# Moving the first loads of a fused attention and two-layer MoE kernel within the program's order

## The chip, the cores and the metric

The kernel runs on one core of one Trainium2 chip. The metric is the device time of one execution in microseconds (us). The program before took 1236.12 us (median of three runs, 1235.98 to 1238.45).

Engines, as the profile names them: PE is TensorE's matrix multiply and PEld its weight load, DVE is VectorE, ACT is ScalarE, POOL is GpSimd, SP is SyncE, which here issues nearly all DMA transfers.

## The reference, cut

Attention with normalized queries and keys over 4 batches and 12 heads of 448 positions and 64 channels, then two feed-forward layers on the 1792 tokens of 768 channels:

```python
def attention(q, k, v, g_q, g_k):                    # (4, 12, 448, 64)
    q_n, k_n = rmsnorm(q, g_q), rmsnorm(k, g_k)      # x / sqrt(mean(x*x) + 1e-6) * g
    s = q_n @ k_n.T / 8
    p = exp(s - max(s)); p = p / (sum(p) + 1e-9)
    return p @ v
x = tokens(attention(...))                           # (1792, 768)
x = relu(x @ w_in) ** 2 @ w_out                      # 768 -> 2048 -> 768
y = ((x @ w1) * (x @ w2)) @ w3 @ w_out2              # 768 -> 1024 -> 1024 -> 768
```

The feed-forward weights arrive as 64-bit floating-point words. The kernel multiplies w3 and w_out2 first (the product is called w3o) and then uses the product as one matrix.

## The kernel before, in words

**Passes.** The main loop (L676) runs over 48 heads in four passes of 12, one pass for each batch. While a pass computes the attention of its heads, a generator gives out matmuls that fill TensorE between them: in the first pass `gen_w3o` (the product w3o), in the later ones `gen_moe` of the batch before. `fill(n)` takes about n matmuls from the generator; six calls of it stand in each turn of the loop.

**Weight units.** The weights are cut into units of 128 rows and 384 or 512 columns, 384 to 512 KB as 64-bit words. For each unit there is a load (L180, buffer raw64, four of them), `words` (on ACT the exponent part, L194; the low word on POOL, L200, or every third unit in the first pass on ACT, L198), `join` on DVE (L207), `split_hi` on ACT (the fp32r half, L106) and `split_lo` on POOL or, every fifth unit in the first pass, on DVE (the rest, L114). `mm3` (L262 to L264) then makes three matmuls for each weight block and operand: high by high, high by low, low by high. In the first product both operands are such units: unit 0 is from w3, units 1 to 4 are from w_out2 and are kept in tiles x and act, unit 5 is from w3 again. `advance` gives out the steps some units ahead: loads five units ahead, words three, joins two.

**Heads.** Four heads are a group. `load_group` loads natural-order keys kn (two buffers) and queries qn (one buffer) of a group; `group_prep` makes their sums of squares (ACT L450, DVE L452) and reciprocal roots (DVE L428 to L434, tile rr). `load_head` loads one head's transposed queries qt (two buffers), `load_v` its values. `head_prep` makes kx and its halves khl on POOL, qh on ACT and ql on DVE (L496). `stage_k` transposes the keys (L508), `stage_qk` makes scores for half a head and their maxima (L524 to L527, tile nb), `stage_exp` the exps on ACT (L543), `stage_t` and `stage_lo` the transposed probabilities, `stage_v` the product with the values.

**Order.** The text of the program gives each instruction its rank; the framework then plans one queue for each engine from ranks, readiness and free buffers, and each engine works through its queue in order, waiting where it must. So an instruction that is ready early may stand ahead of the program's text, and a load stands in SP's queue behind others that wait.

**The start.** L661 to L675: the gains, group 0 (with the first head's keys and queries and units 0 and 1 in between, L397 to L403), the second head's queries (L663), then `group_prep(0)`, the third head's queries (L671), `head_prep(1)` and the first values (L673). The first turn of the loop issues the fourth head's queries, the second values and group 1 (L678 to L681), and only the `fill` at L683 reaches unit 2.

Of the kernel before, what the change touches and what calls it, by code (L numbers as in the profile page):

```python
# [29 lines left out]
def attention_moe_kernel(  # L30
# [19 lines left out]
    GH = 4  # L50
# [120 lines left out]
    def is64(i):  # L171
        return units[i][0].dtype != F32
# [14 lines left out]
    def load_to(i):  # L187
        while pos["load"] <= min(i, NU - 1) and is64(pos["load"]):
            load_next()
# [200 lines left out]
    def load_group(g):  # L390
        if not (0 <= g < NH // GH):
            return
        b, h0 = divmod(g * GH, H)
        qn = t1.tile([P, GH, C, D], F32, name="qn", tag="qn")
        kn = t2.tile([P, GH, C, D], F32, name="kn", tag="kn")
        if g == 0:
            nc.sync.dma_start(out=kn[:, 0:1], in_=k_nat[0, :, 0:1])  # L397
            load_head(0)
            nc.sync.dma_start(out=qn[:, 0:1], in_=q_nat[0, :, 0:1])
            load_to(0)  # L400
            nc.sync.dma_start(out=kn[:, 1:], in_=k_nat[0, :, 1:GH])
            nc.sync.dma_start(out=qn[:, 1:], in_=q_nat[0, :, 1:GH])
            load_to(1)  # L403
        else:
            nc.sync.dma_start(out=kn, in_=k_nat[b, :, h0:h0 + GH])
            nc.sync.dma_start(out=qn, in_=q_nat[b, :, h0:h0 + GH])
        grp[g] = [qn, kn, None, None]

    def load_head(h):
        if not (0 <= h < NH):  # L410
            return
        b, hh = divmod(h, H)
        t = t2.tile([128, S], F32, name="qt", tag="qt")
        nc.sync.dma_start(out=t, in_=q_t[b, hh])
        qts[h] = t

    def load_v(h):
        if not (0 <= h < NH):
            return
        b, hh = divmod(h, H)  # L420
        t = t2.tile([128, C, D], F32, name="v", tag="v")
        nc.sync.dma_start(out=t, in_=v_in[b, hh])
        vs[h] = t
# [105 lines left out]
    def stage_exp(h, s):  # L529
        if not (0 <= h < NH):  # L530
            return
        d = heads[h]
        nb, o = d.pop("nb"), d.pop("sc")
        i = h % 2
        if s == 0 and i == 0:
            sums2[h // 2] = small.tile([P, 2, C], F32, name="sm", tag="sm")
        sm = sums2[h // 2]
        c0 = 2 * s
        pp = t3.tile([P, 2, S], F32, name="p", tag="p")
        for j in range(2):  # L540
            c = c0 + j
            p = d["p"][c] = pp[:, j, :]
            nc.scalar.activation(  # L543
                out=p, in_=o[j], func=AF.Exp, scale=d["rq"][:, c:c + 1], bias=nb[:, j:j + 1],
                accum_out=sm[:, i, c:c + 1],
            )
        if h >= H:
            words = t3.tile([P, 2, S], F32R, name="pw", tag="pw")
            nc.sync.dma_start(out=words.bitcast(F32), in_=pp)
            d["p"][c0:c0 + 2] = [words[:, 0, :], words[:, 1, :]]  # L550
        if s == 1 and i == 1:
            nc.vector.tensor_scalar(out=sm, in0=sm, scalar1=1e-9, scalar2=None, op0=ALU.add)
            rs = small.tile([P, 2, C], F32, name="rs", tag="rs")
            nc.vector.reciprocal(out=rs, in_=sm)
            wide = t1.tile([P, C, 2, D], F32, name="rsw", tag="rsw")
            nc.gpsimd.tensor_scalar(
                out=wide, in0=rs.rearrange("p i c -> p c i").unsqueeze(3).to_broadcast([P, C, 2, D]),
                scalar1=1.0, scalar2=1.0, op0=ALU.mult, op1=ALU.mult,
            )
            sums2[h // 2] = wide.rearrange("p c i d -> p c (i d)")  # L560
# [84 lines left out]
    def start_fill(gen, total):  # L645
        state.update(gen=gen, credit=0.0, left=total)
# [14 lines left out]
    nc.sync.dma_start(out=g_sb, in_=g_in)  # L661
    load_group(0)
    load_head(1)  # L663
    make_identity(nc, ident)
    nc.vector.tensor_copy(out=ident_r, in_=ident)
    nc.vector.scalar_tensor_tensor(
# [8 lines left out]
    first.close()  # L675
    for h in range(NH + 1):  # L676
        n = W3O / ((H + 1) * 6) if h <= H else MOE / (H * 6)
        load_head(h + 3)  # L678
        load_v(h + 1)
        if h % GH == 0:  # L680
            load_group(h // GH + 1)  # L681
        stage_qk(h, 0)
        fill(n)  # L683
        stage_exp(h, 0)
        if h % H != 1:
            stage_x(h - 2)
        stage_t(h - 1, 0)
        stage_t(h - 1, 1)
        fill(n)
        stage_lo(h - 1)  # L690
        if h < NH:
            v_prep(h)
        fill(n)
        stage_k(h + 1)
        stage_t(h - 1, 2)
        stage_t(h - 1, 3)
        fill(n)
        stage_lo(h - 1)
        stage_qk(h, 1)
        fill(n)  # L700
        stage_exp(h, 1)
        fill(n)
        stage_v(h - 1)
        if h % GH == 1:
            group_prep(h // GH + 1)
        head_prep(h + 2)
        if h and h % H == 0:
            fill(1e9)
            stage_x(h - 1)
            start_fill(gen_moe(h // H - 1), MOE)  # L710
# [57 lines left out]
```

## Time and profile before

| | us |
|---|---|
| median of three runs | 1236.12 |
| the profiled execution | 1234.55 |
| its span, first to last instruction | 1232.8 |
| PE busy in the span | 1160.9 (94%) |
| ACT busy | 728.5 (59%) |
| DVE busy | 709.7 (58%) |
| POOL busy | 781.3 (63%) |

A share over the whole span says little here: the first 450 us (the start, the first pass and most of the second) and the rest have different limits. A table of stretches shows for each stretch how long each engine was busy, the granted clock of TensorE and how busy the DMA engines were. A table of waits shows for one engine what released it and how long it stood idle for that. A timeline shows single instructions with start, duration, and, in brackets, idle time before them with what ended it.

### The profile page before, as it was taken

The page shows a single profiled execution, that of the slowest core. Times are in us where ns is not written, and L with a number is a line of the kernel's source. Part 1 is how long each engine was busy: PE and PEld are TensorE (multiplying, and loading weights), DVE is VectorE, ACT ScalarE, POOL GpSimd, SP SyncE. Part 2 cuts the span into 40 slices and gives each one's busy share as a digit, 9 for nine tenths or more (in the row PEclk, how much of TensorE's full clock was granted, in tenths as well). Part 3 has the DMA queues.
Part 4 walks back from the last instruction along what each step waited for, and adds up shares of the span by engine and source line. Part 5 has one row for each costly group of instructions (what it writes and reads, how often), then busy time and mean ns, then how long its engine had stood idle before and what let it go on. Part 6 is the DMA issues. An engine that isn't in the chain of part 4 may idle for free.

```text
span 1232.8 us, 18950 instructions
## 1 busy us (share of the span) xinstructions
PE 1160.9 (94%) x6192; PEld 1049.3 (85%) x6192; DVE 709.7 (58%) x1314; ACT 728.5 (59%) x1553; POOL 781.3 (63%) x772
## 2 busy tenths in 40 slices
PE   3789999998989899999999999999999999999998
PEld 2578888886878789998998998999999999999998
DVE  6699879768978774646567555655664421012100
ACT  5889876767657565656645555656545554343342
POOL 5875534655676655766776764856766556678673
PEclk9999999999998999999999999999999999999999
DMA  7774557888888755555535455544544443333342
GB/s 218 244 238 151 165 146 226 276 283 264 251 264 257 234 180 179 146 148 145 151 118 161 139 169 158 143 142 127 154 123 120 138 138 113 107 116 102 104 125 75
DMA packets 111347, 207.63 MB, mean 168 GB/s; under 512 B 12208, under 2 KB 66704, under 8 KB 111248
## 3 DMA queue, kind: packets, MB, share of 16 engines
q1 hardware_dynamic: 107792, 200.92, 54.0%
q10 hardware_dynamic: 3456, 5.51, 1.2%
q8 instruction: 49, 0.80, 0.3%
q14 instruction: 50, 0.41, 0.1%
HBM read 149.95 MB, written 27.53 MB: 144 GB/s over the span
## 4 chain that ended last, share of the span: by engine, by line
PE 60%; DMA 4%; DVE 2%; POOL 2%; ACT 1%; issue 1%; SPq 0%; DVEq 0%; POOLq 0%; ACTq 0%
PE mm L262 17%; PE mm L263 17%; PE mm L264 17%; PE kv L622 3%; PE pt L570 3%; DMA raw<-w 2%; DMA pw<-p 2%; PE sc L525 1%; PE sc L524 1%; POOL hl L114 1%; DVE raw L207 1%; PE kv L508 1%; PE mm L611 0%; ACT p L543 0%; POOL x L114 0%
## 5 line engine op out<-in xcount | busy, mean ns | idle before, releaser
L114 POOL TENSOR_TENSOR hl<-raw,hl 128x384 fp32r<-128x384 f32 (+1 forms) x383 | 446.4, 1169 | 258.5 <-ACT hl L106 253.3
L106 ACT ACTIVATE hl<-raw 128x384 fp32r<-128x384 f32 (+1 forms) x416 | 233.7, 564 | 147.6 <-PE mm L264 85.6
L263 PE MATMUL mm<-x,hl 128*128 128x448 f32 (+1 forms) x832 | 306.2, 368 | 8.6 <-POOL x L114 8.6
L262 PE MATMUL mm<-x,hl 128*128 128x448 f32 (+1 forms) x832 | 310.5, 373 | 3.8 <-ACT x L106 1.8
L264 PE MATMUL mm<-x,hl 128*128 128x448 f32 (+1 forms) x832 | 305.7, 367 | 4.5 <-POOL hl L114 2.6
L263 PE MATMUL mm<-act,hl 128*128 128x448 f32 (+1 forms) x640 | 234.4, 366 | 3.3 <-POOL act L114 3.2
L262 PE MATMUL mm<-act,hl 128*128 128x448 f32 (+1 forms) x640 | 236.9, 370 | 0.0
L264 PE MATMUL mm<-act,hl 128*128 128x448 f32 (+1 forms) x640 | 233.6, 365 | 0.7 <-DVE hl L114 0.7
L543 ACT ACTIVATE p<-sc,nb,rr 112x448 f32<-112x448 f32 x192 | 137.4, 719 | 86.4 <-DVE nb L527 83.0
L263 PEld LDWEIGHTS mm<-x,hl 128*128 128x128 f32 x832 | 158.1, 190 | 22.1 <-POOL x L114 10.2
L264 PEld LDWEIGHTS mm<-x,hl 128*128 128x128 f32 x832 | 158.2, 190 | 19.0 <-POOL hl L114 4.0
L262 PEld LDWEIGHTS mm<-x,hl 128*128 128x128 f32 x832 | 157.9, 190 | 18.5 <-ACT x L106 3.3
L526 DVE TENSOR_REDUCE nb<-sc 112x1 f32<-112x448 f32 x192 | 113.1, 615 | 35.6 <-PE sc L525 34.3
L263 PEld LDWEIGHTS mm<-act,hl 128*128 128x128 f32 x640 | 121.0, 189 | 14.3 <-POOL act L114 4.8
L264 PEld LDWEIGHTS mm<-act,hl 128*128 128x128 f32 x640 | 120.9, 189 | 10.6 <-DVE hl L114 1.1
L262 PEld LDWEIGHTS mm<-act,hl 128*128 128x128 f32 x640 | 121.0, 189 | 9.4
L114 DVE TENSOR_TENSOR ptr<-pt,ptr 128x448 fp32r<-128x448 f32 x144 | 87.1, 619 | 72.0 <-ACT ptr L106 71.4
L200 POOL TENSOR_SCALAR raw<-raw 128x384 uint32<-128x384 uint16 (+1 forms) x110 | 82.1, 747 | 73.0 <-DMA raw<-w_in 18.8
L207 DVE SCALAR_TENSOR_TENSOR raw<-raw 128x384 uint32<-128x384 uint32 (+1 forms) x120 | 84.8, 711 | 39.8 <-POOL hl L114 25.2
L194 ACT ACTIVATE raw<-raw 128x384 f32<-128x384 f32 (+1 forms) x120 | 70.5, 597 | 53.9 <-DMA raw<-w 18.0
L114 POOL TENSOR_TENSOR act<-gf,act 128x448 fp32r<-128x448 f32 x80 | 97.4, 1218 | 7.2 <-DVE gf L334 3.0
L334 DVE TENSOR_TENSOR gf<-mm,r 128x448 f32<-128x448 f32 x64 | 39.8, 621 | 94.4 <-ACT r L330 93.9
(82 smaller groups left out, 1588.7 us busy)
## 6 DMA issues: line engine op xcount, KB each, us to landing
pw<-p SPq DMA_DIRECT2D x72, 392.0 KB, 4.3
raw<-f_in SPq DMA_DIRECT2D x96, 192.0 KB, 2.4
raw<-f_out SPq DMA_DIRECT2D x72, 256.0 KB, 2.7
raw<-f SPq DMA_DIRECT2D x96, 192.0 KB, 2.4
raw<-w_in SPq DMA_DIRECT2D x32, 384.0 KB, 4.5
raw<-w_out SPq DMA_DIRECT2D x24, 512.0 KB, 6.1
raw<-w SPq DMA_DIRECT2D x32, 384.0 KB, 4.9
raw<-w3o SPq DMA_DIRECT2D x48, 256.0 KB, 2.7
```

What stands on the lines that cost most here:

```text
L106: nc.scalar.activation(out=out, in_=in_, func=AF.Copy)
L114: e.tensor_tensor(out=out, in0=in0, in1=in1, op=ALU.subtract)
L194: nc.scalar.activation(out=hi, in_=hi, func=AF.Prelu, scale=2.0**-112, alpha=-(2.0**32))
L200: nc.gpsimd.tensor_scalar(out=t[:, :n, 0], in0=low, scalar1=2.0**-13, scalar2=2.0**-14 - 0.5, op0=ALU.mult, op1=ALU.add)
L207: nc.vector.scalar_tensor_tensor(out=f[:, :n].bitcast(U32), in0=t[:, :n, 1], scalar=3, in1=t[:, :n, 0], op0=ALU.logical_shift_left, op1=AL ...
L262: nc.tensor.matmul(ps, w[:, 0, wk, :], x[0], start=(i == 0), stop=False)
L263: nc.tensor.matmul(ps, w[:, 0, wk, :], x[1], start=False, stop=False)
L264: nc.tensor.matmul(ps, w[:, 1, wk, :], x[0], start=False, stop=(i == last))
L334: nc.vector.tensor_tensor(out=gf, in0=ps, in1=r, op=ALU.mult)
L526: nc.vector.tensor_reduce(out=nb[:, j:j + 1], in_=o[j], axis=AX.X, op=ALU.max, negate=True)
L543: nc.scalar.activation(out=p, in_=o[j], func=AF.Exp, scale=d["rq"][:, c:c + 1], bias=nb[:, j:j + 1], accum_out=sm[:, i, c:c + 1],)
L570: nc.tensor.transpose(to[:kn, c * P:(c + 1) * P], d["p"][c][:, k0:k0 + kn], one)
```

## The change

Four places in the program's text:

- units 2 and 3 are loaded directly behind the second head's queries (`load_to(3)`);
- in the first turn of the loop the second values, group 1 and the fourth head's queries are issued behind `stage_exp(0, 0)` instead of ahead of `stage_qk(0, 0)`;
- groups from group 2 on are loaded in the turns h = 3, 7, 11, ... instead of 4, 8, 12, ...;
- `head_prep(h + 2)` stands ahead of `group_prep`, no longer behind it.

No instruction is added or taken away.

```diff
@@ -661,6 +661,7 @@
     nc.sync.dma_start(out=g_sb, in_=g_in)
     load_group(0)
     load_head(1)
+    load_to(3)
     make_identity(nc, ident)
@@ -675,13 +676,18 @@
     for h in range(NH + 1):
         n = W3O / ((H + 1) * 6) if h <= H else MOE / (H * 6)
-        load_head(h + 3)
-        load_v(h + 1)
-        if h % GH == 0:
-            load_group(h // GH + 1)
+        if h:
+            load_head(h + 3)
+            load_v(h + 1)
+            if h % GH == 3:
+                load_group(h // GH + 2)
         stage_qk(h, 0)
         fill(n)
         stage_exp(h, 0)
+        if h == 0:
+            load_v(1)
+            load_group(1)
+            load_head(3)
         if h % H != 1:
             stage_x(h - 2)
@@ -701,9 +707,9 @@
         stage_v(h - 1)
+        head_prep(h + 2)
         if h % GH == 1:
             group_prep(h // GH + 1)
-        head_prep(h + 2)
         if h and h % H == 0:
             fill(1e9)
```

## Rows read from the trace of the kernel before

**Rows 1.** Stretches: us; each engine's busy time (instructions), clock, DMA share, GB/s.

```profile
10.00:20.00 10.00, 3.81 (x10) 2.06 (x10) 9.61 (x31) 4.14 (x9) 5.04 (x6) 1.00 0.92 276
20.00:30.00 10.00, 4.76 (x18) 3.04 (x18) 5.24 (x9) 6.62 (x14) 9.08 (x13) 1.00 0.49 164
30.00:60.00 30.00, 21.25 (x87) 15.96 (x88) 20.15 (x33) 24.41 (x55) 24.79 (x25) 0.94 0.77 243
60.00:120.00 60.00, 54.18 (x329) 48.20 (x327) 58.67 (x112) 53.39 (x114) 41.13 (x47) 1.00 0.63 197
...
180.00:450.00 270.00, 242.11 (x1265) 214.65 (x1265) 219.09 (x398) 176.97 (x386) 163.35 (x177) 0.97 0.80 250
450.00:1230.00 780.00, 777.40 (x4135) 713.25 (x4133) 343.13 (x612) 411.31 (x869) 508.38 (x463) 1.00 0.46 134
```

**Rows 2.** Waits of PE, 0 to 60 us: total us, times, longest us.

```profile
PE mm L263 <- POOL x L114: 7.3, 4, 2.9
PE sc L524 <- ACT p L543: 3.4, 1, 3.4
PE mm L263 <- POOL act L114: 3.2, 4, 1.7
PE mm L262 <- ACT x L106: 1.8, 1, 1.8
```

**Rows 3.** Timeline of PE: start us, duration us, engine, line, operation, [idle before, releaser].

```profile
29.95 0.69 PE L263 MATMUL mm<-x,hl 128*128 128x384 f32 x1 [2.91 <-POOL x L114]
```

**Rows 4.** Timeline of SP's issues, first 17 us.

```profile
4.47 2.85 SPq L414 DMA_DIRECT2D qt<-q_t  x2
...
8.32 0.44 SPq L405 DMA_DIRECT2D kn<-k_nat  x1
12.24 0.32 SPq L406 DMA_DIRECT2D qn<-q_nat  x1
...
14.96 1.37 SPq L180 DMA_DIRECT2D raw<-wo  x3
```

**Rows 5.** Timeline of ACT, 18 to 64 us.

```profile
18.99 0.72 ACT L543 ACTIVATE p<-sc,nb,rr 112x448 f32<-112x448 f32 x1 [5.68 <-DVE nb L527]
...
23.04 0.54 ACT L194 ACTIVATE raw<-raw 128x384 f32<-128x384 f32 x1
...
25.80 0.51 ACT L106 ACTIVATE x<-raw 128x384 fp32r<-128x384 f32 x1
...
63.43 1.05 ACT L450 ACTIVATE qn<-kn 112x1024 f32<-112x1024 f32 x1
```

**Rows 6.** Timeline of POOL, 10 to 20 us.

```profile
10.66 0.68 POOL L200 TENSOR_SCALAR raw<-raw 128x384 uint32<-128x384 uint16 x1 [1.20 <-DMA raw<-wo]
...
14.01 1.37 POOL L114 TENSOR_TENSOR x<-raw,x 128x384 fp32r<-128x384 f32 x1
17.16 1.58 POOL L114 TENSOR_TENSOR vhl<-v,vhl 128x256 fp32r<-128x256 f32 x2 [1.78 <-DVE nt L432]
19.85 0.61 POOL L480 TENSOR_TENSOR kx<-kn,rr 112x256 f32<-112x256 f32 x1 [1.11 <-issue]
```

**Rows 7.** Timeline of DVE, 6 to 15 us.

```profile
6.29 0.69 DVE L496 SCALAR_TENSOR_TENSOR ql<-qt,gg,qh 128x448 fp32r<-128x448 f32 x1
...
12.20 0.55 DVE L207 SCALAR_TENSOR_TENSOR raw<-raw 128x384 uint32<-128x384 uint32 x1
...
12.83 1.70 DVE L496 SCALAR_TENSOR_TENSOR ql<-qt,gg,qh 128x448 fp32r<-128x448 f32 x1
```

**Rows 8.** Timeline of all engines around a kn load and a group's square.

```profile
85.18 0.63 POOL L480 TENSOR_TENSOR kx<-kn,rr 112x256 f32<-112x256 f32 x1
...
85.84 0.33 SPq L405 DMA_DIRECT2D kn<-k_nat  x1
...
176.22 1.06 ACT L450 ACTIVATE qn<-kn 112x1024 f32<-112x1024 f32 x1 [3.64 <-DMA kn<-k_nat]
...
178.04 0.46 PE L524 MATMUL sc<-kt,qh 128*112 128x448 f32 x1 [1.62 <-ACT p L543]
```

## Prediction

> **What bounds the kernel now.** I read the table of stretches first, then the waits of TensorE (PE) in the stretches where it stands idle, and last the order of each engine's instructions there. The table says where PE idles [rows 1]. From 450 us on it is busy 777.4 of 780 us: no wait of another engine ends last there. From 180 to 450 us it idles 27.9 us, with DMA busy 0.80 of the time. From 60 to 120 us it idles 5.8 us, but VectorE (DVE) is busy 58.67 of 60. From 10 to 60 us it idles 10 − 3.81, 10 − 4.76 and 30 − 21.25, together 20.2 us. The reader should see that in these 50 us no engine is full throughout: DVE is full from 10 to 20 us (9.61 of 10) and about half busy in the next ten, GpSimd (POOL) is half idle from 10 to 20 us (5.04) and full in the next ten (9.08), and ScalarE (ACT) does 4.14 of 10 in the first stretch. Work is short there, then comes all at once.
>
> What is short are weight units. Each unit (64-bit words) is made into an fp32 value and split into two fp32r halves by ACT (exponent, sometimes the low word, high half), POOL (low word, low half) and DVE (join). The waits of PE in the first 60 us that name a unit are 7.3 us for low halves in tile x, 3.2 us for those in tile act and 1.8 us for a high half [rows 2]. The longest, 2.9 us, ends at 29.95 us: it is for unit 2's low half, and the 1.8 us a little earlier for the same unit's high half [rows 2, 3]. Unit 2's load was issued at 14.96 us, behind group 1's two loads at 8.32 and 12.24 us [rows 4]. Its exponent was begun on ACT at 23.04 us, and before that ACT had stood 5.68 us, to 18.99 us, for the first exp's bias [rows 5], and POOL 1.78 and 1.11 us ahead of its work at 17.16 and 19.85 us [rows 6]. Both engines idled with no unit to work on, although two of the four unit buffers had never been used.
>
> **The change, part by part.**
>
> 1. *Units 2 and 3 behind the second head's queries.* Two issues move from 14.96 us to directly behind the first load of the pair at 4.47 us [rows 4]. Queued behind them on SP are now the third head's queries and the first value tile: two issues of about 0.45 us (1.37 us for three [rows 4]), and 768 KB in the data, at the 276 GB/s of the stretch from 10 to 20 us [rows 1] an estimated 2.8 us. Unit 1 lands at 10.66 us, where POOL's wait for it ends [rows 6]; behind it come 224 KB of queries and 384 KB for each unit, so units 2 and 3 land at an estimated 12.9 and 14.3 us, and the third head's queries and the values 1.3 us later, at 15.6 us. The values are read by POOL from 17.16 us on [rows 6]: covered, 0; without that cover up to 2.8 us, on the work on the values alone.
>    What moves into idle time: on ACT two exponents of 0.54 us, one low word, put at the same 0.54, and two high halves of 0.51, together 2.6 us, into the wait of 5.68 us [rows 5]. On POOL one low word of 0.68 and two low halves of 1.37 us, together 3.4 us, against 1.78 + 1.11 = 2.9 us of idle time [rows 6]. On DVE two joins of 0.55 us [rows 7], into a stretch that is already full.
>    POOL is the fullest engine after it (9.08 of 10, then 24.79 of 30 us [rows 1]), so the gain is what POOL does ahead of time: 2.9 us. The bounds: at the top the two waits of PE for unit 2 are all gone, 1.8 + 2.9 = 4.7 us; with units 4 and 5 earlier too (their buffers come free with the joins, the second of which ends at 12.75 us [rows 7], and a group load no longer stands in the queue ahead of them) ACT's whole 5.7 us could be filled. At the bottom, below nothing: the first exp comes later by 3.1 us (rival 2). I take 2.9 us, by the row of the engine that is full next.
>
> 2. *The first pass's loads (values 1, group 1, queries 3) behind its exps.* Their readers don't wait now: group 1's last square lies at 63.43 us with no wait in front [rows 5], 55 us behind the first of the group's loads. SP may have nothing else to issue behind the units, and then part of them goes out where it goes now. Cost 0, covered by those 55 us; uncovered, a group load that lands late holds ACT as it does at 176.22 us, for 3.64 us, and PE 1.62 us at 178.04 us [rows 8]. What it gives, a queue free for units 4 and 5, is already in the bounds of part 1.
>
> 3. *Groups loaded a head ahead, from group 2 on.* A load of kn needs the buffer of the group before last, which the last kx of that group frees: kx at 85.18 us, load at 85.84 us [rows 8], and so for nine of the eleven groups. For these the buffer and not the place in the program sets the time, so 0, and the wait of 3.64 us stays where it is. Only group 2 can go earlier; its squares have no wait in front, so 0.
>
> 4. *head_prep before group_prep.* No instruction more or less; only the rank of some ACT, DVE and POOL work at every fourth head. For this the trace has no row; I take 0, between − 1.6 and + 1.6 us (one wait of PE as at 178.04 us, either way [rows 8]).
>
> Sum: − 2.9 us. From 60 to 120 us DVE is full, so the gain survives only if DVE gets its work earlier too; from 20 to 60 us it is idle 4.8 + 9.9 = 14.6 us [rows 1], so it has the room. After that every stage is the same, begun 2.9 us earlier. Against the profiled execution: 1234.55 − 2.9 = 1231.7 us (its span is 1232.8, with 1.75 us around it). The median of the three runs lies 1.57 us above that execution, so 1236.12 − 2.9 = **1233.2 us**.
>
> **Rivals.**
>
> 1. *The whole head start, faster.* Units 4 and 5 follow at once, ACT's 5.68 us are filled, and POOL is fed without a gap: − 5.7 us, 1230.4. For it: ACT and POOL work on each unit in turn, and ACT has the time. Against it: POOL has only 2.9 us free there.
>
> 2. *The first exp becomes late, slower.* The chain to the first exp ends on DVE, which is full from 10 to 20 us [rows 1]. Two joins put 2 × 0.55 = 1.1 us into it. Besides, DVE slows while POOL works: the operation that makes ql takes 0.69 us at 6.29 us and 1.70 us at 12.83 us [rows 7], where POOL makes low halves (one from 14.01 us [rows 6]). Each of two more low halves ahead of the exp may so cost DVE 1.0 us. The exp would then start at 18.99 + 1.1 + 2.0 = 22.1 us, 3.1 us later. It decides once the waits for the units are gone and the exps of heads 0 and 1 end last before 60 us. Then nothing is won and up to 3.1 us are lost: 1239.2. Against it: of PE's waits up to 60 us only 3.4 us are for an exp [rows 2].
>    The Trainium skill speaks for this rival: SBUF — State Buffer, section "Who interferes with whom", says that a DVE instruction with two SBUF inputs and a GpSimd instruction that reads SBUF exclude each other for the whole instruction. The trace agrees as far as the 1.70 against 0.69 us go. By the rule alone each low half could hold DVE for its whole 1.37 us, which would make the exp an estimated 3.8 us later instead of 3.1.
>
> 3. *Given back.* The units come earlier, but DVE, full from 60 to 120 us, ends its part no earlier: between 0 and − 1 us, 1235.6. For it: 58.67 of 60 [rows 1]. Against it: DVE's 14.6 idle us before.
>
> 4. *A new order later on.* Parts 3 and 4 change the rank of work at every fourth head. Between 180 and 450 us, where PE idles 27.9 us, three more waits as at 178.04 us cost 4.9 us: 1238.1 with the gain of part 1; three fewer would give 1228.3. Nothing in the trace says which.
>
> 5. *It doesn't do what it says.* For the group loads this is the forecast (buffer, not place). For units 2 and 3 it can hardly be, since their buffers are free; it has no chance of its own.
>
> **How the numbers follow.** 0.2% is 2.5 us, about what a measurement of this kernel can tell from no change. Forecast (− 1.5 to − 4.7 us): 0.40, of it 0.29 beyond 2.5 us. Rival 1: 0.13, faster. Rival 2: 0.13, of it 0.10 slower. Rival 3: 0.14, same. Rival 4: 0.20, of it 0.06 faster, 0.02 same, 0.12 slower. Faster 0.29 + 0.13 + 0.06 = 0.48; same 0.11 + 0.03 + 0.14 + 0.02 = 0.30; slower 0.10 + 0.12 = 0.22. The forecast's own range is 1231.4 to 1234.6. The range that holds 8 in 10 goes down past rival 1 towards rival 4's lower end and up past rival 2: 1227 to 1240.
>
> **What would show it.** Right: units 2 and 3 issued near 5 us, their exponents on ACT before 18 us, the low half of unit 2 in use on PE before 25 us instead of at 29.95, POOL busy more than 6.5 of 10 in the stretch from 10 to 20 us, TensorE's idle time from 10 to 60 us down by about 3 us and that of the later stretches as it is. The first exp later than 21 us shows the cost of rival 2. PE idle from 60 to 120 us by more than 7 us, DVE as full as now, shows rival 3. Loads of kn that no longer follow the last kx, or PE idle from 180 to 450 us away from 27.9 us by more than 2 us, show rival 4. The forecast is wrong if PE's idle time from 10 to 60 us does not fall.

## The result: 0.65% slower

The changed kernel takes 1245.56 us (median of 13 runs, 1239.13 to 1248.99) against 1236.18 us for the kernel before (13 runs, 1233.9 to 1243.29): ratio 1.0065, 95% interval 1.005 to 1.0079. The forecast was 1233.2 us with a range of 1227 to 1240; the sign was wrong, and the time lies 5.6 us above the range. The profiled execution of after took 1244.28 us, its span is 1242.4 us.

**The busy times.** Of the 9.6 us between the spans, TensorE's busy time takes 10.6 (1160.9 to 1171.5 us) for the same 6192 matmuls; DVE (709.7), ACT (728.4) and POOL (778.6) are as busy as before or less. The table of stretches of after (columns as in [rows 1]):

```profile
10.00:20.00 10.00, 4.77 (x13) 2.51 (x12) 9.59 (x28) 6.52 (x13) 5.27 (x6) 1.00 0.77 254
20.00:30.00 10.00, 7.14 (x21) 4.87 (x21) 5.71 (x12) 5.98 (x13) 8.99 (x13) 1.00 0.73 242
30.00:60.00 30.00, 18.03 (x65) 12.78 (x65) 17.39 (x29) 20.75 (x46) 19.05 (x20) 0.93 0.57 179
60.00:120.00 60.00, 54.93 (x314) 48.32 (x315) 53.91 (x107) 50.77 (x105) 40.33 (x44) 0.95 0.72 219
120.00:180.00 60.00, 55.23 (x324) 50.03 (x323) 48.58 (x101) 44.63 (x100) 26.97 (x36) 0.94 0.45 130
180.00:450.00 270.00, 244.96 (x1277) 216.45 (x1276) 219.85 (x402) 178.41 (x390) 160.30 (x178) 0.96 0.79 248
450.00:1230.00 780.00, 777.46 (x4142) 713.45 (x4142) 351.05 (x623) 416.33 (x881) 512.95 (x468) 1.00 0.47 137
```

Against [rows 1], TensorE does more up to 30 us (34 matmuls from 10 to 30 us, 28 before), then much less from 30 to 60 us (65, before 87). From 10 to 60 us it idles 5.23 + 2.86 + 11.97 = 20.1 us, before 20.2: the same idle time with 99 instead of 115 matmuls in it. From 120 to 180 us, where the kernel before had

```profile
120.00:180.00 60.00, 56.94 (x355) 51.63 (x354) 49.47 (x108) 47.16 (x106) 26.10 (x35) 1.00 0.53 155
```

after does 31 matmuls less, at a granted clock of 0.94. From 450 us on the rows are alike. (The profile has no record of the clock before its first rise, at 33.8 us in before and 41.9 in after, and the table counts that time as 1.00; the distance of the matmuls shows the lower level there.)

**The start of after.** Issues on SP, work on ACT, POOL, PE and DVE (each with "..." where rows are left out), and one row of SP's waits from 36 to 47 us:

```profile
5.24 1.69 SPq L180 DMA_DIRECT2D raw<-wo  x2
...
36.95 0.33 SPq L180 DMA_DIRECT2D raw<-wo  x1
41.51 0.38 SPq L289 DMA_DIRECT2D w3o<-osb  x1
41.98 0.44 SPq L414 DMA_DIRECT2D qt<-q_t  x1
46.02 2.99 SPq L180 DMA_DIRECT2D raw<-wo  x4
```
```profile
13.70 0.55 ACT L194 ACTIVATE raw<-raw 128x384 f32<-128x384 f32 x1
...
20.16 0.72 ACT L543 ACTIVATE p<-sc,nb,rr 112x448 f32<-112x448 f32 x1 [0.50 <-DVE nb L527]
...
31.61 0.54 ACT L194 ACTIVATE raw<-raw 128x384 f32<-128x384 f32 x1
34.21 0.52 ACT L106 ACTIVATE act<-raw 128x384 fp32r<-128x384 f32 x1 [2.06 <-DVE raw L207]
...
40.99 0.49 ACT L106 ACTIVATE osb<-mm 128x384 f32<-128x384 f32 x1 [2.24 <-PE mm L264]
...
44.16 1.00 ACT L194 ACTIVATE raw<-raw 128x384 f32<-128x384 f32 x2
```
```profile
22.91 0.85 POOL L480 TENSOR_TENSOR kx<-kn,rr 112x256 f32<-112x256 f32 x1 [0.18 <-DVE rr L434]
...
30.21 1.09 POOL L114 TENSOR_TENSOR khl<-kx,khl 112x256 fp32r<-112x256 f32 x1
31.27 1.26 POOL L114 TENSOR_TENSOR hl<-raw,hl 128x512 fp32r<-128x512 f32 x1
32.50 0.99 POOL L114 TENSOR_TENSOR act<-raw,act 128x384 fp32r<-128x384 f32 x1
...
40.19 1.07 POOL L200 TENSOR_SCALAR raw<-raw 128x384 uint32<-128x384 uint16 x1 [0.96 <-DMA raw<-wo]
47.22 2.30 POOL L114 TENSOR_TENSOR act<-raw,act 128x384 fp32r<-128x384 f32 x2 [5.97 <-ACT act L106]
```
```profile
33.54 0.69 PE L263 MATMUL mm<-act,hl 128*128 128x384 f32 x1 [4.48 <-POOL act L114]
34.03 0.53 PE L264 MATMUL mm<-act,hl 128*128 128x384 f32 x1
34.35 0.53 PE L262 MATMUL mm<-act,hl 128*128 128x384 f32 x1
...
40.43 0.52 PE L264 MATMUL mm<-act,hl 128*128 128x384 f32 x1
```
```profile
30.64 2.86 DVE L527 TENSOR_TENSOR nb<-nb,rr 112x2 f32<-112x2 f32 x1
```
```profile
SPq L180 <- DVE raw L207: 5.8, 2, 3.5
```

What the edit was to do, it did: units 2 and 3 are issued at 5.24 us, unit 2's exponent begins at 13.70 us instead of 23.04 [rows 5], ACT's wait of 5.68 us ahead of the first exp is down to 0.50. But the stretch without a new exponent has not gone, it has moved. Before it lay between

```profile
10.60 0.55 ACT L194 ACTIVATE raw<-raw 128x384 f32<-128x384 f32 x1
```

and 23.04 us (12.4 us), where POOL made the keys of heads 1 to 3 from 19.85 us on [rows 6]. Now it lies between 31.61 and 44.16 us (12.5 us). The steps to it, in the rows: units came first, so those keys come from 22.91 to 31.3 us, with unit work between, and the low half of a unit in tile act stands behind them (32.50); TensorE waits 4.48 us for it and is still at the lower clock level behind that wait (the matmul at 34.35 starts 0.32 us behind the one at 34.03); so the first product ends late for ACT's queue, which holds its copy (40.99, 2.24 us of waiting) ahead of four exponents. Their four units had all landed when POOL took up the low word of the last of them at 40.19 us. They fill the four buffers, so SP issues no unit load between 36.95 and 46.02 us: it waits, 3.5 us at the longest, for the join of the first of the four. The store of the copy (41.51) and the fifth head's queries (41.98), which stand ahead of that load in SP's queue, are not what holds it. POOL idles 5.97 us. DVE has a part in the pause too: the instruction on tile nb, the bias of an exp (L527, 112x2 elements), takes 2.86 us from 30.64 us and ends with POOL's low half (33.49), the join behind it is late, and ACT waits 2.06 us for that join (34.21). By 44 us 14 exponents have begun in the kernel before and 10 in after.

**From 124 to 165 us.** POOL, SP, ACT, DVE and PE of after (chosen rows):

```profile
134.48 0.61 POOL L480 TENSOR_TENSOR kx<-kn,rr 112x256 f32<-112x256 f32 x1
135.12 0.33 SPq L405 DMA_DIRECT2D kn<-k_nat  x1
138.93 1.06 ACT L450 ACTIVATE qn<-kn 112x1024 f32<-112x1024 f32 x1 [1.66 <-DMA kn<-k_nat]
139.90 0.71 ACT L543 ACTIVATE p<-sc,nb,rr 112x448 f32<-112x448 f32 x1
140.75 0.46 PE L524 MATMUL sc<-kt,qh 128*112 128x448 f32 x1 [1.51 <-ACT p L543]
...
162.55 0.56 ACT L194 ACTIVATE raw<-raw 128x384 f32<-128x384 f32 x1 [2.06 <-DMA raw<-w_in]
163.19 0.47 DVE L527 TENSOR_TENSOR nb<-nb,rr 112x2 f32<-112x2 f32 x1
163.70 0.72 ACT L543 ACTIVATE p<-sc,nb,rr 112x448 f32<-112x448 f32 x1 [0.60 <-DVE nb L527]
164.57 0.58 PE L524 MATMUL sc<-kt,qh 128*112 128x448 f32 x1 [1.94 <-ACT p L543]
```

Twice an operation that needs a transfer stands in ACT's queue directly ahead of an exp: the keys' square 3.8 us after its load's issue, later a unit's exponent. At the square ACT waits for the data, the exp behind it is late, and TensorE waits 1.51 us. At 163.70 us it is DVE that ends last: the unit's exponent is done at 163.11, but the bias that the exp needs only at 163.66, and TensorE waits 1.94 us. In the kernel before the same square came 6.2 us after its load, with no wait:

```profile
128.39 0.33 SPq L405 DMA_DIRECT2D kn<-k_nat  x1
...
134.63 1.07 ACT L450 ACTIVATE qn<-kn 112x1024 f32<-112x1024 f32 x1
```

The load still follows the last kx of the group (134.48, 135.12), as in [rows 8]; not the load moved, but ACT's order around it. The later wait of [rows 8] (3.64 us) is still there:

```profile
187.90 1.06 ACT L450 ACTIVATE qn<-kn 112x1024 f32<-112x1024 f32 x1 [3.75 <-DMA kn<-k_nat]
```

**A table by work done.** Stretches of equal time compare unequal work once a kernel is late, so I counted the sets of three matmuls (L262 to L264; 1472 in all, the first 128 are the product w3o) by the start of their third one, and took the time between the same sets in each trace, us. Three executions of each kernel are shown (the later two are from e5 to e8 below).

| kernel | to set 16 | 16 to 74 | 74 to 103 | 103 to 128 | 128 to 407 | 407 to end |
|---|---|---|---|---|---|---|
| before | 55.9, 56.6, 56.7 | 68.5, 69.1, 69.3 | 33.1, 32.6, 32.7 | 28.1, 28.2, 30.0 | 266.1, 263.3, 265.4 | 777.0, 777.1, 776.6 |
| after | 62.8, 62.5, 63.3 | 68.6, 68.6, 68.9 | 38.0, 36.7, 38.0 | 27.9, 28.2, 27.9 | 264.6, 266.8, 265.2 | 776.5, 777.5, 775.7 |
| difference of means | +6.5 | −0.3 | +4.8 | −0.8 | +0.6 | −0.3 |

The last column ends with the last set. The loss lies in two places: the start (+6.5) and about 125 to 165 us (+4.8). From set 128 on (about 186 us in before) nothing is lost, although 29.6 of the 68.2 us that TensorE idles up to its last matmul in the first profile of before lie there. The differences add up to 10.5 us where the ratio says 8.0: the traced executions of before (1234.55, 1232.68 and 1236.56 us) are mostly faster than its median.

### The profile page after: what moved, and what is told of

Same layout as the page of the kernel before. It is cut to its first block, busy times and chain, and to the rows that moved or that the text cites. A ratio compares the mean times of both kernels' runs of the same rounds, so it can differ in the third digit from the quotient of the medians.

```text
span 1242.4 us, 18949 instructions
## 1 busy us (share of the span) xinstructions
PE 1171.5 (94%) x6192; PEld 1056.4 (85%) x6192; DVE 709.7 (57%) x1314; ACT 728.4 (59%) x1553; POOL 778.6 (63%) x772
## 4 chain that ended last, share of the span: by engine, by line
PE 60%; DMA 5%; DVE 2%; POOL 2%; ACT 1%; issue 1%; SPq 0%; DVEq 0%; POOLq 0%; ACTq 0%
PE mm L262 17%; PE mm L263 17%; PE mm L264 17%; PE kv L622 3%; PE pt L570 3%; DMA pw<-p 2%; DMA raw<-w 2%; PE sc L525 1%; PE sc L524 1%; POOL hl L114 1%; DMA kn<-k_nat 1%; PE kv L508 1%; POOL x L114 0%; PE mm L611 0%; DVE raw L207 0%
## 5 line engine op out<-in xcount | busy, mean ns | idle before, releaser
L262 PE MATMUL mm<-x,hl 128*128 128x448 f32 (+1 forms) x832 | 310.6, 373 | 0.7 <-ACT x L106 0.5
L264 PE MATMUL mm<-x,hl 128*128 128x448 f32 (+1 forms) x832 | 306.7, 369 | 3.8 <-DVE hl L114 2.2
L263 PE MATMUL mm<-act,hl 128*128 128x448 f32 (+1 forms) x640 | 237.0, 370 | 6.9 <-POOL act L114 6.7
L262 PE MATMUL mm<-act,hl 128*128 128x448 f32 (+1 forms) x640 | 239.7, 374 | 0.4 <-ACT act L106 0.4
L264 PE MATMUL mm<-act,hl 128*128 128x448 f32 (+1 forms) x640 | 235.5, 368 | 0.3 <-DVE hl L114 0.3
L264 PEld LDWEIGHTS mm<-x,hl 128*128 128x128 f32 x832 | 158.4, 190 | 19.1 <-POOL hl L114 3.7
L262 PEld LDWEIGHTS mm<-x,hl 128*128 128x128 f32 x832 | 158.2, 190 | 14.7 <-ACT x L106 1.8
L263 PEld LDWEIGHTS mm<-act,hl 128*128 128x128 f32 x640 | 122.4, 191 | 18.8 <-POOL act L114 9.4
L526 DVE TENSOR_REDUCE nb<-sc 112x1 f32<-112x448 f32 x192 | 113.5, 616 | 38.1 <-PE sc L525 36.7
L262 PEld LDWEIGHTS mm<-act,hl 128*128 128x128 f32 x640 | 122.5, 191 | 10.9 <-ACT act L106 1.2
L264 PEld LDWEIGHTS mm<-act,hl 128*128 128x128 f32 x640 | 122.4, 191 | 10.5 <-DVE hl L114 0.7
L200 POOL TENSOR_SCALAR raw<-raw 128x384 uint32<-128x384 uint16 (+1 forms) x110 | 78.8, 716 | 82.8 <-DMA raw<-w_in 23.2
L207 DVE SCALAR_TENSOR_TENSOR raw<-raw 128x384 uint32<-128x384 uint32 (+1 forms) x120 | 78.1, 654 | 47.6 <-POOL hl L114 25.5
```

Of the source, the lines that this page charges most:

```text
L200: nc.gpsimd.tensor_scalar(out=t[:, :n, 0], in0=low, scalar1=2.0**-13, scalar2=2.0**-14 - 0.5, op0=ALU.mult, op1=ALU.add)
L207: nc.vector.scalar_tensor_tensor(out=f[:, :n].bitcast(U32), in0=t[:, :n, 1], scalar=3, in1=t[:, :n, 0], op0=ALU.logical_shift_left, op1=AL ...
L262: nc.tensor.matmul(ps, w[:, 0, wk, :], x[0], start=(i == 0), stop=False)
L263: nc.tensor.matmul(ps, w[:, 0, wk, :], x[1], start=False, stop=False)
L264: nc.tensor.matmul(ps, w[:, 1, wk, :], x[0], start=False, stop=(i == last))
L526: nc.vector.tensor_reduce(out=nb[:, j:j + 1], in_=o[j], axis=AX.X, op=ALU.max, negate=True)
```

## The experiments

Two theories stood at the end of the reading. **Places**: the two places of the table, each with its cause in the queues. **Clock**: counting the upper-level time (columns / 2.4 GHz) of the matmuls that started while the granted clock was at 1.2 GHz, which is also what they lost by it, gives 14.1, 13.9 and 14.0 us for three executions of before and 23.2, 26.0 and 21.5 for after, that is, +9.6 of the +10.5 us between the mean spans; so the lower clock level behind long waits could be the whole loss. Where it lies speaks against that already: 3.5 of the 9.6 us lie before set 16 and 0.9 between sets 74 and 103, but 2.6 between 16 and 74 and 3.0 between 128 and 407, where nothing is lost.

### One step at a time

Each ratio is against runs of the kernel before beside the same experiment (their medians: 1238.10 us for e1 to e4, 1236.50 for e9 to e12, 1237.52 for e13 to e15, 1236.64 for e16 to e18).

**e1: units 2 and 3 early, nothing else.**

```diff
     load_head(1)
+    load_to(3)
```

> The first step alone: units 2 and 3 behind the second head's queries, all else as before. The theory that the start loses by queue order (units then stand behind the first product's store and the fifth head's queries on SP, and ScalarE's copies of units stand ahead of head 1's keys) expects that this step alone already makes the start late: the 30th low-by-high matmul near 71 to 73 us instead of 66.9, total 3 to 6 us slower than before. The rival, that the loads behind the exps are what makes it late, expects the 30th such matmul at 64 to 67 us and a total of 0 to 4 us faster.

Measured: 1241.73 us, ratio 1.0038 (1.0011 to 1.0064).

**e2: the first pass's loads behind its exps.**

```diff
-        load_head(h + 3)
-        load_v(h + 1)
-        if h % GH == 0:
-            load_group(h // GH + 1)
+        if h:
+            load_head(h + 3)
+            load_v(h + 1)
+            if h % GH == 0:
+                load_group(h // GH + 1)
...
         stage_exp(h, 0)
+        if h == 0:
+            load_v(1)
+            load_group(1)
+            load_head(3)
```

> The second step alone: values 1, group 1 and the fourth head's queries behind the first exps, units 2 and 3 where they were in the text. If this step makes the start late: the 30th low-by-high matmul after 70 us and a total 3 to 6 us slower. If it is the units' step that does: within 2.5 us of before. If it takes both together: each alone within 2.5 us.

Measured: 1239.62 us, 1.0028 (1.0013 to 1.0043).

**e3: groups a head ahead.**

```diff
-        if h % GH == 0:
-            load_group(h // GH + 1)
+        if h == 0:
+            load_group(1)
+        if h % GH == 3:
+            load_group(h // GH + 2)
```

> The third step alone: groups from group 2 on loaded a head ahead. The prediction's reason (the buffer and not the place in the program sets the time) expects no difference, under 2.5 us. The theory that the second loss, 5.5 us between heads 6 and 10 (102 to 170 us of before), comes from this step's new ranks expects 3 to 6 us slower, lost between 100 and 180 us, with nothing lost before 70 us.

Measured: 1241.69 us, 1.0044 (1.0025 to 1.0064).

**e4: head_prep ahead of group_prep.**

```diff
+        head_prep(h + 2)
         if h % GH == 1:
             group_prep(h // GH + 1)
-        head_prep(h + 2)
```

> The fourth step alone: head_prep ahead of group_prep. The prediction put it at 0 within 1.6 us. The theory that the second loss (5.5 us, heads 6 to 10) comes from this step expects 3 to 6 us slower with the loss from 65 us on; the rival, that a late start alone shifts everything, expects both this run and the groups' run within 2.5 us of before.

Measured: 1241.45 us, 1.0024 (1.0005 to 1.0043).

**e16 and e17: the change in two halves**, e1 with e2, and e3 with e4 (the diffs together).

> Steps 1 and 2 alone (units 2 and 3 early, first pass's loads behind its exps); groups and head_prep as in the kernel before. Step 1 alone measured 1.0038, step 2 alone 1.0028. Theory 'TensorE's time is paid in full wherever it is added, so what counts is how many waits of about 2 us the new queues hold and when the clock first rises': as in the changed kernel the unit loads stand behind the first product's store at 37 to 46 us, so the first rise comes at 40 us or later, and the time is 1.003 to 1.006 of before. Rival 'the steps add up': 1.0066 or more. Rival 'step 1 is good and only its companions cost': 1.002 or less.

Measured: 1253.71 us, 1.013 (1.0107 to 1.0153): nearly twice the 0.66% of steps that add up.

> Steps 3 and 4 alone (groups a head ahead, head_prep ahead of group_prep); the start as in the kernel before, so the first rise at 33 to 36 us and the falls up to 60 us as before. Theory 'TensorE's time is paid in full': what it is longer by comes from waits of TensorE of about 2 us near 120 and 160 us with the lower level behind them: 1.002 to 1.005 of before. Rival 'the start sets it all': within 0.002 of before. Rival 'the steps add up': 1.0068.

Measured: 1242.84 us, 1.0043 (1.0027 to 1.0059).

Each step costs by itself, and the costs do not add: the four ratios sum to 1.34%, the halves to 1.73%, the whole costs 0.65%. The table by work done says where (one execution each; after and before are the means of three; most of the single ones were slower than their kernel's median, e3's took 1245.60 us against 1241.69):

| kernel | to set 16 | 16 to 74 | 74 to 103 | 103 to 128 | 128 to 407 | 407 to end |
|---|---|---|---|---|---|---|
| before | 56.4 | 69.0 | 32.8 | 28.8 | 264.9 | 776.9 |
| e1, units | 61.5 | 65.4 | 36.5 | 29.7 | 266.2 | 777.7 |
| e2, loads | 61.8 | 65.0 | 37.6 | 28.3 | 266.3 | 776.6 |
| e16, start | 63.4 | 76.1 | 36.9 | 28.4 | 265.6 | 777.5 |
| e3, groups | 58.3 | 69.6 | 39.7 | 27.8 | 266.7 | 777.6 |
| e4, prep | 59.4 | 69.0 | 34.8 | 29.6 | 266.3 | 777.0 |
| e17, later | 57.8 | 69.4 | 38.7 | 29.6 | 266.8 | 777.3 |
| after | 62.9 | 68.7 | 37.6 | 28.0 | 265.5 | 776.6 |

To set 16, every kernel with step 1 or 2 is 5 to 7 us late. But alone each step makes most of it good by set 74, which e1 and e2 reach at 126.9 and 126.8 us, against 125.3 in before and 131.6 in after: the start's loss stays only where both are made (e16 and after), and what e1 and e2 cost lies mostly between sets 74 and 103. Nor do the two go the same way. In e2 the pause in the exponents has moved as in after (31.8 to 43.1 us). In e1 it stays in its old place (13.8 to 28.0 us), by 44 us 14 exponents have begun as in before, set 14 comes at 52.4 us (54.1 in the first trace of before), and what makes set 16 late is two waits of TensorE for low halves in tile x:

```profile
57.49 0.45 PE L263 MATMUL mm<-x,hl 128*128 128x384 f32 x1 [3.29 <-POOL x L114]
...
61.01 0.69 PE L263 MATMUL mm<-x,hl 128*128 128x384 f32 x1 [2.31 <-POOL x L114]
```

In e3, e4 and e17 set 16 comes 1.4 to 3.0 us late, though up to 60 us every queue in them has the order of the kernel before; their first unit's exponent came 1.0, 1.9 and 0.5 us later in these executions, which e18 (below) shows for the kernel before too. Between sets 74 and 103 every kernel here whose queues ahead of it were planned anew loses something, 2.0 to 6.9 us. In e3 the waits of ACT and PE from 126 to 168 us (total us, times, longest) are the kinds that after has, for the keys and for a bias:

```profile
ACT p L543 <- DVE nb L527: 3.2, 2, 2.7
...
ACT qn L450 <- DMA kn<-k_nat: 2.9, 1, 2.9
```
```profile
PE sc L524 <- ACT p L543: 4.2, 2, 2.4
```

and e16, without steps 3 and 4, has the square's wait too (3.6 us between 138 and 176 us). In e1 the same place has another wait: 2.6 us of TensorE for a low half of the probabilities.

```profile
PE pt L570 <- DVE ptr L114: 3.1, 2, 2.6
```

So it is not one bad edit. e16 loses another 7 us between sets 16 and 74, where after loses none. Its row of TensorE's waits there (60 to 126 us) is

```profile
PE pt L570 <- DVE ptr L114: 4.0, 2, 3.5
```

and steps 3 and 4, which alone cost 0.43%, take this away. Why the framework's plan of e16 places this wait I did not find out.

### The two kernels again

No edit: further executions of both, to see what of a trace repeats.

> The kernel before, unchanged, profiled a second time. The clock theory (the change loses because TensorE works more of its time at the lower of its two clock levels) expects the work that TensorE does at that level to be less than in the changed kernel: 10 to 18 us worth at full clock, and a mean granted clock of 0.987 to 0.992. If the first trace of before was merely a lucky one, it is 20 us or more here.

> The changed kernel, unchanged, profiled a second time. The clock theory expects 20 to 26 us worth of TensorE's work done at the lower level, and the rest of the time that is not work the same as before within 2 us. The theory of a worse order expects the rest to be 4 to 9 us longer than in before, whatever the clock did.

> The kernel before, a third profile: as for the second, 10 to 18 us worth of work at the lower level by the clock theory.

> The changed kernel, a third profile: as for the second, 20 to 26 us worth at the lower level by the clock theory; 4 to 9 us more of other lost time by the theory of a worse order.

Measured: before 1232.68 and 1236.56 us, after 1246.47 and 1245.11. The first rise of the clock came at 33.8, 35.1 and 33.8 us in before, at 41.9, 40.8 and 42.5 in after. Both places of the table repeat in all three pairs.

### Zero matmuls in TensorE's waits

To see whether the clock behind the waits is a cause, matmuls with a tile of zeros were added to TensorE's order. They keep it active and add zeros to the sum. (The edits are shortened here; each kernel also makes the zero tile `zr`, one DVE instruction. `idle` is 2 in the first eighth of the product in e9 and e10, 1 in all of it in e11 and e12.)

```diff
     def mm3(ps, w, wk, x, i, n, idle=0):
         nc.tensor.matmul(ps, w[:, 0, wk, :], x[0], start=(i == 0), stop=False)
+        for _ in range(idle): nc.tensor.matmul(ps, zr, x[0], start=False, stop=False)
```

**e9 and e10**: 32 of them, early.

> The kernel before, with two matmuls of a zero tile put behind the first of each set of three in the first eighth of the weight product (16 sets, 32 matmuls of 384 columns, added into the same PSUM tile, so they add zeros): they run while TensorE waits for the next half of a unit, so that it stands idle less before its clock has risen. At the upper clock level they are 32 x 0.16 = 5.1 us of work, mostly inside the 20 us that TensorE idles from 10 to 60 us. Theory 'the clock sets the loss': the first rise comes earlier than 33.8 us and the work done at the lower level falls below the 14 us of the kernel before; the time is between 4 us less and 2 us more than before. Rival 'late units set the loss': the clock changes nothing that ends last, and the time is the same or up to 5 us longer.

Measured: 1240.54 us, 1.0032 (1.0016 to 1.0048).

> The changed kernel with the same 32 zero matmuls. Theory 'the clock sets the loss': the work done at the lower level falls from 21.5 to 26 us towards that of the kernel before with the fillers, and the time from 1245 us to within 4 us of that kernel. Rival 'late units set the loss': units, queries and keys are as late as in the changed kernel, so it stays 8 to 10 us longer than the kernel before with the same fillers, whatever the clock does.

Measured: 1242.55 us, 1.0043 (1.0027 to 1.0059).

Between the two kernels 2 us are left of 9. In after the 5.1 us of extra work come with no longer time (1.0043 of before against 1.0065 without them, with intervals that overlap). In after the clock now rises at 23.0 us, and the time to set 16 falls from 62.9 to 59.1 us (in before it grows from 56.4 to 58.0). This speaks for the clock in the start, but not cleanly: the other queues were planned anew too (between sets 74 and 103 the kernel before now takes 37.3 us, like after).

**e11 and e12**: 128 of them, in the whole product.

> The kernel before with one zero matmul in each of the 128 sets of three of the whole weight product: 128 x 0.16 = 20.5 us more of work for TensorE at the upper level, spread to about 190 us, where it idles 20 + 6 us and some between 120 and 180 us. Theory 'the clock sets the loss': the falls of the clock up to 190 us are gone or shorter; the time is longer than before by 5 to 20 us, the filler work that finds no idle time. Rival: as much longer, the falls as before.

Measured: 1261.22 us, 1.0191 (1.0164 to 1.0219).

> The changed kernel with the same 128 zero matmuls. Theory 'the clock sets the loss': the gap to the kernel before with the same fillers shrinks from 9 us to under 4 us, because both run the first 190 us at the same level. Rival 'late units set the loss': the gap stays 8 to 10 us.

Measured: 1268.23 us, 1.0246 (1.0216 to 1.0276).

The gap is 7 us, between the two forecasts (under 4, and 8 to 10), 3.6 of them to set 16 (57.8 and 61.4 us). Between sets 74 and 103 both take 39.0 and 39.1 us: with 4.6 us more matmuls there the difference is gone.

**e13, e14 and e15**: the same, at named sets from 300 us on, where the order of the other matmuls stays in e13 and e14 (e15 adds 20 at the sets 99, 180 and 233).

```diff
-        nc.tensor.matmul(ps, w[:, 0, wk, :], x[0], start=(i == 0), stop=False)
+        nc.tensor.matmul(ps, w[:, 0, wk, :], x[0], start=(i == 0), stop=False)
+        for _ in range({257: 7, 261: 6, 313: 10, 328: 4, 366: 4, 370: 4, 396: 4}.get(set, 0)):
+            nc.tensor.matmul(ps, zr, x[0], start=False, stop=False)
```

> The kernel before, with 39 matmuls of a zero tile (39 x 0.187 = 7.3 us at the upper level) at seven places between 300 and 445 us, behind the first matmul of the sets of three with the numbers 257, 261, 313, 328, 366, 370 and 396, where TensorE waited 1.3 to 2.4 us in the profiles of the kernel before and four or five stretches of 3.4 us at the lower clock level began (at 306.8, 361.4, 375.1 and 443.4 us; 5 x 3.4 / 2 = 8.5 us of loss). The order of the other matmuls stays. Theory 'a long wait costs its length and the clock behind it': at most one of these stretches is left, the fillers lie in the waits, and the time falls by 3 to 8 us, to 1228 to 1233 us. Rival 'only the wait counts, the lower clock is a symptom': the waits are filled with work that does nothing, and the time stays within 2 us or grows by up to 7 us.

Measured: 1243.69 us, 1.0048 (1.0031 to 1.0066).

> The changed kernel with the same 39 zero matmuls at the same seven places. Theory 'a long wait costs its length and the clock behind it': the falls at 329, 373 and 390 us go (4 x 3.4 / 2 = 6.8 us) and the time comes down by 3 to 8 us to 1237 to 1242 us; what is left over the kernel before with the same fillers is the late first rise of the clock and the falls at 59, 120, 165, 250 and 298 us, 7 to 10 us. Rival: it stays at 1245 us or is up to 7 us longer.

Measured: 1254.64 us, 1.0124 (1.0106 to 1.0141).

> As the last, with 20 more zero matmuls at the sets 99, 180 and 233, where the changed kernel waited 1.9 to 2.6 us ahead of the falls at 165, 250 and 298 us. Theory 'a long wait costs its length and the clock behind it': three more falls go, and the time comes down by another 3 to 5 us, to 1233 to 1238 us, about the kernel before. Rival: no further gain, or longer by up to 4 us, the work of the 20 fillers.

Measured: 1259.24 us, 1.0174 (1.0158 to 1.019).

These three speak against the clock as the whole cause. Between sets 128 and 407 in e14 the work done at the lower level falls from 9.5 us (the first execution of after) to 4.8, as the theory wants, yet the stage grows from 264.6 to 272.0 us, by all of the 7.3 us of added matmuls; in e13 from 266.1 to 275.0. The idle time between these sets hardly shrank in e13 (27.9 to 26.9 us) and grew in e14 (24.7 to 26.6). By themselves these runs don't decide, since ACT, DVE, POOL and SP were planned in another order behind the first filling (from about 310 us in e13 and 323 in e14). But kernels without a filling say the same. In this stage what the lower level costs and what TensorE idles replace each other: 8.0 + 27.9 = 35.9, 6.7 + 25.3 = 32.0 and 5.0 + 28.6 = 33.6 us in the three executions of before, 34.2, 35.9 and 34.7 in after, 35.8 in e2, with 12.2 us at the lower level, and 34.8 in e16, with 6.4. The stage's length does not follow its clock: it is 263.3 us with 6.7 us at the lower level, 265.4 with 5.0, 264.6 with 9.5 and 266.3 with 12.2. A slow matmul there takes the place of a wait.

**e18: the control**, the zero tile made but not used.

> The kernel before with the zero tile of the filling runs made (one VectorE instruction of 128x128 more at the start) and no zero matmul; every queue otherwise in the same order. Both theories: within 0.15% of before, 1234.5 to 1238.5 us; the work at the lower level 13 to 17 us. If it is 0.3% or more longer, the filling runs can't be read as the price of the zero matmuls.

Measured: 1237.02 us, 0.9999 (0.9983 to 1.0015). So the tile costs nothing. In its profiled execution the first exponent began 1.1 us later than in the first profile of before, the clock first rose at 40.3 us instead of 33.8, and the time to set 16 was 58.3 us, with every queue in the order of the kernel before apart from that one instruction. A rise at 40.3 us, with that later beginning, goes with about 2 us there, not 6.5.

**Order or clock in the start.** Up to 60 us the queues of e3, e4, e13, e17 and e18 have the order of the kernel before, and their clocks differ. They lose 8.5 to 10.0 us to the lower level before set 16 (e3 10.0, e4 9.9), where before loses 6.1 to 7.2 and after 9.5 to 10.9, and reach that set at 57.6 to 59.4 us; after reaches it at 62.5 to 63.3, in e14 and e15 too, which have its order there. So a clock as in after, with the order of before, makes set 16 1.9 us late in e3 and 3.0 in e4, of which the later beginning is 1.0 and 1.9. The greater part of the 6.5 us comes with the order.

No version beat the kernel before.

## Why the prediction was wrong, point by point

1. **"Behind the second head's queries": units 2 and 3.** Issue (5.24 us) and exponents (13.70 us for unit 2's) came as foretold. The low half of unit 2 was in use at 19.96 us, before the 25 us that I named. The step that failed is the size of the gain, "what POOL does ahead of time: 2.9 us", and with it "after that every stage is the same, begun 2.9 us earlier". POOL was costed as a sum of free and busy time. It is a queue in order, and its idle time was not filled: from 10 to 20 us it is busy 5.27 us, before 5.04, where I had named more than 6.5. In after, unit work put ahead of the keys of heads 1 to 3 pushed them from 19.85 to 22.91 us and the next unit's low half to behind them at 32.50 us, and through the 4.48 us wait and the first product's copy in ACT's queue the pause in the exponents came back at 31.61 to 44.16 us. The term was −2.9. Alone (e1) the step gains nothing: set 16 comes at 61.5 us against 56.4, by two waits for low halves and without that pause, set 74 at 126.9 against 125.3, and the whole is 0.38% longer. Why steps 1 and 2, each nearly made good by set 74 alone, cost 6 us there together (131.6) is open. The prediction's own sign of failure, "if PE's idle time from 10 to 60 us does not fall", came true: 20.1 against 20.2 us.
2. **First pass's loads behind its exps, cost 0.** Wrong: e2 costs 5.4 us to set 16, most of it made good by set 74, and 0.28% in all. The 55 us of cover were right for the readers of group 1. What was left out is that the moved issues are not the only thing that changes: with them out of SP's queue the unit loads follow sooner, and the start has the same pause in the exponents (31.8 to 43.1 us in e2) as after.
3. **Groups a head ahead, cost 0.** The reason given held where it was read from, and there the load follows the last kx (134.48, 135.12 us). It does not hold "for nine of the eleven groups": in the trace of before it does for seven, and the kn loads at 275.58 and 372.88 us come 25 and 20 us behind that kx. The cost was not 0: 0.44% alone, lost between sets 74 and 103, where the square on ACT stands ahead of an exp. I priced where the load goes out and not where its reader now stands.
4. **head_prep ahead of group_prep, 0 within 1.6 us either way.** Alone it costs 0.24% (0.05 to 0.43), 3.0 us by the ratio: beyond the 1.6 us I gave, though the interval reaches below that.
5. **Rival 4, a new order later on**, was right in its mechanism: waits as at 178.04 us [rows 8]. But they came at 125 to 165 us, where I had looked for no loss, and without part 1's gain to set against them; hence the time above its 1238.1. That its price, 4.9 us for three more, is about what that stage lost (4.8) is chance: TensorE waits there three times for an exp, 4.4 us in all, where before it waits twice, 1.3 us, and 0.9 us of the loss is clock. TensorE's idle time from 180 to 450 us, named as the sign of it, went from 27.9 to 25.0 us while that stage stayed as long: I had put the sign in the wrong stretch, and idle time alone does not measure it.
6. **Rival 2, a late first exp.** It came at 20.16 us, 1.2 us late and not 3.1 (in e18, with no load moved, at 20.22). DVE did hold the chain, but later: by the bias of 2.86 us at 30.64 us. The queues that decided were POOL's and ACT's. **Rival 3, given back**: the head start was indeed given back, before 60 us, in the queues of POOL and ACT and not in DVE's after it, and set 16 came 6.5 us later.

What is shown: the two places, the waits in them, that the start's loss stays only where steps 1 and 2 are both made (one execution for each step), and that the order and not the lower clock makes the greater part of it. What is only argued: the chain from POOL's queue to the pause, since no run moved one of its links alone, and how much the lower clock behind the 4.48 us wait adds. The matmuls before set 16 lost some 3.5 us more by it in after than in before; e10 gives back 3.8, with other queues changed; e3 and e4 put it at 3.0 or less.

## What to carry to other kernels

In a kernel whose queues are planned from ranks, a moved load is priced at every queue that is planned anew, not at the load: after an early start, look for the pause that it removed further down the same chain, and for every operation that waits for a transfer directly ahead of one that another engine needs. Compare two traces by work done, not by stretches of time, and with more than one cut: e1 is 5 us late at set 16 and 1.6 at set 74. And a sum of lost clock that equals the loss is no cause: look stage by stage whether the length follows it.

## What the runs showed of the hardware

**The clock often falls behind single waits.** In the profiles of before and after the clock fell from its upper level more than once after TensorE had stood idle once for about 2 us in otherwise full work (behind the wait of 1.94 us that ends at 164.57 us it fell at 164.7 us). Not each such wait was followed by a fall: of those of 1.75 us and more behind the first rise, 3 of 6, 3 of 5 and 4 of 8 in three executions of before, and 6, 6 and 4 of 8 in after. And there are falls without such a wait (at 375.1 and 443.4 us in the first profile of before).

**Small DVE instructions stretch to the end of a GpSimd one.** DVE and POOL of after (chosen rows):

```profile
13.89 1.87 POOL L114 TENSOR_TENSOR hl<-raw,hl 128x512 fp32r<-128x512 f32 x1 [1.47 <-ACT hl L106]
13.91 0.67 DVE L496 SCALAR_TENSOR_TENSOR ql<-qt,gg,qh 128x448 fp32r<-128x448 f32 x1
14.51 1.27 DVE L432 TENSOR_TENSOR nt<-rr 112x4 f32<-112x4 f32 x1
17.94 0.15 DVE L432 TENSOR_TENSOR nt<-rr 112x4 f32<-112x4 f32 x1
18.66 1.25 POOL L114 TENSOR_TENSOR x<-raw,x 128x384 fp32r<-128x384 f32 x1 [1.22 <-ACT x L106]
18.95 0.98 DVE L434 SCALAR_TENSOR_TENSOR rr<-nt,rr 112x4 f32<-112x4 f32 x1
```

An operation of 0.15 us takes 1.27 us and ends at 15.78, when POOL's ends (15.76); another ends at 19.93, with POOL's at 19.91; the bias of 2.86 us above ends at 33.50, with POOL's third operation in a row (33.49). This agrees with the rule that the prediction weighed (the Trainium skill, SBUF — State Buffer, section "Who interferes with whom"): a DVE instruction with two SBUF inputs and a GpSimd instruction that reads SBUF exclude each other for the whole instruction. The cost lands on the smallest instructions of a chain, where I had looked for it on the large one, whose second instance took 1.70 us before [rows 7] and 0.67 us here, where it is POOL's operation beside it that takes long (1.87 us at 13.89, 1.26 at 31.27).
